# Moving the second MoE's weight conversion one half block later, and sixteen low-part subtractions from GpSimd to VectorE

## The chip, the core and the metric

The kernel runs on one core of a Trainium2 chip. The metric is device microseconds of one execution; lower is better.

## The reference

A linear attention feeds two MoE layers. There are 4 batches of 8 heads, 576 rows and 64 columns a head, which make 2304 tokens of 512 features; each MoE goes 512 to 2048 to 512.

```python
q_s = softmax(q, over the head's columns); k_s = softmax(k, over the rows)
x = q_s @ (k_s^T @ v)                          # per batch and head, then heads side by side
h = x @ moe_w_in;  g = where(h >= 1, h, where(h <= -1, 0, (h + 1)**2 / 4));  x = g @ moe_w_out
h = x @ moe2_w_in; g = h * tanh(log1p(exp(h)));                              out = g @ moe2_w_out
```

## The kernel before

The first MoE goes over the tokens in six blocks (0 to 5) of 384 columns. Each block has 16 slots, one for each 128 of the 2048 hidden features, so slots are counted from 0 to 95 through all blocks. In slot i TensorE makes gemm1 of feature group i (lines 496 to 498, 12 matmuls into a PSUM bank h) and gemm2 of group i - 3 (line 582, 12 matmuls into four banks acc). Block 0 multiplies in whole float32. From block 1 on each operand is split into a high part that is rounded and a low part that is the rest, and three products are summed. `act_scaled`, `act_squared` and `act_least` make g from h (ScalarE lines 539 and 543, VectorE line 548); `split_g` makes the high part of g on ScalarE (line 533) and the low part on the engine that `eltwise` names (line 534). There are two h banks, so gemm1 of group i waits until VectorE's line 548 has read group i - 2.

Beside this run four other streams. In block 1 `w_high` and `w_low` split the first MoE's weights (lines 237 and 242; the output weights' low part on GpSimd, the input weights' on VectorE). In blocks 1 to 4 a list of stages (`Fill`) makes the attention of the next block: transposes into qT, ScalarE's copy qt (line 460), and the product xps (line 467). The second MoE's weights are converted once, 32 items (2 matrices by 16 groups). An item is loaded (line 137 or 139), then goes through stages, one for each call of `w_tick`: `first` (two bit operations on VectorE, lines 151 and 155, two passes on ScalarE, 162 and 166), `second` (ScalarE line 170, and the product of line 183, on GpSimd for the input matrix and on VectorE for the output matrix); every second item goes on with `sums` (two additions on VectorE and one on GpSimd), `last_sum` (GpSimd) and `store` (four DMAs to DRAM, line 215, together 896 KB). `w_tick` takes a new item in two slots of three.

In block 5 (slots 80 to 95) the second MoE is made ready. The jobs of `ahead2` do, in this order of slots: 80 `x_load` of group 0 (four DMAs xq, line 665), 81 `x_sums` of group 0 (four additions of 128x768 on GpSimd), 82 `x_store` of group 0 (xk, line 676) and the fetch of converted weights of unit 0 (w, line 633), 83 `x_load` of group 1, 84 `x_sums` of group 1 and the next fetch of weights, 85 `x_store` of group 1 and the first operand (xf, line 685). Within a slot `w_tick` comes first, then gemm1, then these jobs, then `split_g` of the group before and the activations of this slot.

The order of instructions: SyncE, which issues the DMAs, and ScalarE keep the program's order everywhere. TensorE, VectorE and GpSimd are ordered by a planner in slots 16 to 79, and keep the program's order in slots 0 to 15 and from slot 80 on.

After block 5 the second MoE runs on the sums of a fast matrix scheme (lines 496 to 498 into m, then line 783 into o).

Of the kernel before, what the change touches and what calls it, by code (L numbers as in the profile page):

```python
# [63 lines left out]
def tile_attention_two_moes(  # L64
# [13 lines left out]
    nc = tc.nc  # L78
# [4 lines left out]
    NF = DFF // P  # L83
    NB = NT // TB
# [149 lines left out]
    def w_high(c, m):  # L234

        t = parts[c, m] = big([P, 2, DM], F32R, "parts")
        nc.scalar.activation(out=t[:, 0, :], in_=whole[m, c // 2][:, c % 2, :], func=AF.Copy)

    def w_low(c, m):
        t, w = parts[c, m], whole[m, c // 2][:, c % 2, :]  # L240
        eng = nc.gpsimd if m else nc.vector
        eng.tensor_tensor(out=t[:, 1, :], in0=w, in1=f(t[:, 0, :]), op=ALU.subtract)
# [260 lines left out]

    def eltwise(s):

        return nc.vector if s == slots[-1] else nc.gpsimd

    def gemm1(s):
        ph, n, c = s
        hs[s] = h_p.tile([P, 512], F32, tag="h", name="h")  # L510
        for kc in range(NP):
            ks = slice(kc * P, (kc + 1) * P)
            if n == 0:
                nc.tensor.matmul(
                    hs[s][:, :TB], whole[0, c // 2][:, c % 2, ks], xh[ph, n][kc // 2][:, kc % 2, :],
                    start=kc == 0, stop=kc == NP - 1,
                )
                continue
            three(
                hs[s][:, :TB], parts[c, 0][:, 0, ks], parts[c, 0][:, 1, ks],  # L520
                xh[ph, n][kc // 2][:, kc % 2, :], xl[ph, n][kc // 2][:, kc % 2, :], kc == 0, kc == NP - 1,
            )
# [4 lines left out]
    def split_g(s):  # L527
        if as_whole(s):
            return
        g = temps.pop(s)  # L530
        t = small([P, 2, TB], F32R, "ghl")
        gh[s], gl[s] = t[:, 0, :], t[:, 1, :]
        nc.scalar.activation(out=gh[s], in_=g, func=AF.Copy)  # L533
        eltwise(s).tensor_tensor(out=gl[s], in0=g, in1=f(gh[s]), op=ALU.subtract)  # L534
# [28 lines left out]
    def gemm2(s):  # L563
        ph, n, c = s
        first, last = c == 0, c == NF - 1
        key = s[:2]
        if first:
            acc[key] = [acc_p.tile([P, 512], F32, tag="acc", name="acc") for _ in range(NP)]
        if as_whole(s):
            for x, a in enumerate(acc[key]):  # L570
                nc.tensor.matmul(
                    a[:, :TB], whole[1, c // 2][:, c % 2, x * P:(x + 1) * P], gh[s], start=first, stop=last
                )
            del gh[s], hs[s]
            return
        woh, wol = parts[c, 1][:, 0, :], parts[c, 1][:, 1, :]

        order = [(x, at) for ats in ((0, 1), (2,)) for x in range(NP) for at in ats]
        for x, at in order:
            xs = slice(x * P, (x + 1) * P)  # L580
            pairs = [(woh[:, xs], gh[s]), (wol[:, xs], gh[s]), (woh[:, xs], gl[s])]
            nc.tensor.matmul(  # L582
                acc[key][x][:, :TB], *pairs[at], start=first and at == 0, stop=last and at == 2
            )
        del gh[s], gl[s], hs[s]
# [3 lines left out]
    def finish_block(ph, n):  # L589
        for e, a in enumerate(acc.pop((ph, n))):  # L590
            y = yp.tile([P, TB], F32, tag=f"y{e % 2}", name="y")
            if e % 2:
                nc.vector.tensor_copy(y, a[:, :TB])
            else:
                nc.scalar.activation(out=y, in_=a[:, :TB], func=AF.Copy)
            stores.append((yd[n][:, e, :], y))
# [301 lines left out]
    line = Line()  # L898
    fill = None

    def w_ahead():
        while ahead and len(raws) < 1:
            w_load(*ahead.pop(0))

    def w_tick(new):
        line.tick(w_stages(*todo.pop(0)) if todo and new else None)
# [46 lines left out]
    slots = [(1, n, c) for n in range(NB) for c in range(NF)]  # L953
# [7 lines left out]
    def slot(i):  # L961
        nonlocal fill
        s = slots[i] if i < len(slots) else None
        d = slots[i - LAG] if LAG <= i < len(slots) + LAG else None
        if s:
            ph, n, c = s
            if c == 0:
                fill = Fill(*plan.get((ph, n), ([], 1)))
            if (n > 1 or n == 1 and c >= NF // 2) and (n < NB - 1 or line.items):
                w_tick(i % 3)  # L970
                w_ahead()
            if n == 1:
                w = [(x, m) for x, m in ((c + AHEAD, 0), (c, 1)) if x < NF]
                for x, m in w:
                    w_high(x, m)
                for x, m in w:
                    w_low(x, m)
            gemm1(s)
        for job in ahead2.pop(i, []):
            job()  # L980
        while stores:
            nc.sync.dma_start(out=stores[0][0], in_=stores.pop(0)[1])
        for back in (1, 2, 0):
            if 0 <= i - back < len(slots):
                if back < len(acts) and i - back >= NF:
                    acts[back](slots[i - back])
        if fill:
            fill.step()
        if d:
            gemm2(d)  # L990
            if d[2] == NF - 1:
                finish_block(*d[:2])
        if fill:
            fill.step()
            if s and s[2] == NF - 1:
                fill.drain()
# [61 lines left out]
    for engines, upto in REGIONS:  # L1058
        with region(engines):
            for i in range(at, upto):  # L1060
                slot(i)
        at = upto
    with region(None):
        slot(len(slots) + LAG)
        for g in groups:
            for u in units:
                at = (g * len(units) + u) * per_unit
                for x, job in zip((2, 2, 5, 5), unit(g, u, places)):
                    if at + per_unit < end:
                        places.setdefault(at + per_unit + x, []).insert(0, job)  # L1070
                    else:
                        job()
        for at in range(len(products)):
            product(at, steps)
        assert not (todo or line.items or ahead2 or places or steps)
# [32 lines left out]
```

## Time and profile before

| | |
|---|---|
| median of 3 runs | 873.01 us (871.52 to 873.29) |
| the profiled execution | 872.6 us |
| its span, first to last instruction | 870.8 us |
| TensorE busy | 853.1 us (98% of the span) |
| VectorE, ScalarE, GpSimd busy | 563.0, 493.9, 400.5 us |

The profiled execution's own time is 1.8 us over its span and 0.4 us under the median. A matmul is counted as busy until its modelled end, and the next one starts before that, so the start times of matmuls tell more than the busy share.

### The profile page before, as it was taken

To read this page: it belongs to the slowest core of one execution; us is meant where nothing else is said; L and a number is where in the kernel's file an instruction comes from. 1 tells how busy PE (TensorE), PEld (TensorE's weight loads), DVE (VectorE), ACT (ScalarE), POOL (GpSimd) and SP (SyncE) were. 2 spreads that over 40 slices of the span, in tenths; PEclk is the share of its full clock that TensorE was granted. 3 is DMA by queue.
4 is the path that set the end of the run, shared out by engine and by line. 5 is a ranking of instruction groups with operands and counts; after the bars stand their busy time and mean duration, and the time that the engine had idled before them with its cause. 6 is when DMAs were issued, how large, how long until landed. Compare 5 with 4: busy or idle time off the path is not lost. (4 is left out here: it accounts for less than half of the span.)

```text
span 870.8 us, 14851 instructions
## 1 busy us (share of the span) xinstructions
PE 853.1 (98%) x5276; PEld 807.0 (93%) x5276; DVE 563.0 (65%) x907; ACT 493.9 (57%) x849; POOL 400.5 (46%) x373
## 2 busy tenths in 40 slices
PE   9999999989999999999999999999999999999998
PEld 9755769979999999999999999989999999999998
DVE  5899836686775775693147447755777679666453
ACT  2797986586676667784458434433433455553521
POOL 2454636496565355473374226558555467000000
PEclk9999999999999999999999999999999999999999
DMA  9999103225973755562187057687877897867833
GB/s 233 299 292 245 32 1 95 70 68 145 238 210 114 220 149 184 165 230 67 49 296 278 20 194 254 199 314 294 286 247 247 305 354 260 258 231 213 304 115 95
DMA packets 139995, 171.24 MB, mean 197 GB/s; under 512 B 57361, under 2 KB 109585, under 8 KB 139921
## 3 DMA queue, kind: packets, MB, share of 16 engines
q1 hardware_dynamic: 139680, 170.10, 61.6%
q8 instruction: 41, 0.67, 0.3%
q14 instruction: 34, 0.27, 0.1%
q10 hardware_dynamic: 240, 0.20, 0.1%
HBM read 108.40 MB, written 61.87 MB: 196 GB/s over the span
## 5 line engine op out<-in xcount | busy, mean ns | idle before, releaser
L582 PE MATMUL acc<-ghl,parts 128*128 128x384 f32 x960 | 183.0, 339 | 0.0
L582 PEld LDWEIGHTS acc<-ghl,parts 128*128 128x128 f32 x960 | 167.5, 188 | 1.1
L783 PE MATMUL o<-w2p,gc 128*128 128x256 f32 x1296 | 153.2, 280 | 1.7 <-ACT gc L624 1.7
L783 PEld LDWEIGHTS o<-w2p,gc 128*128 128x128 f32 x1296 | 152.5, 189 | 2.1 <-ACT gc L624 2.1
L534 POOL TENSOR_TENSOR ghl<-rg,ghl 128x384 fp32r<-128x384 f32 x79 | 87.9, 1114 | 99.8 <-ACT ghl L533 85.7
L548 DVE SCALAR_TENSOR_TENSOR rg<-h,rg 128x384 f32<-128x384 f32 x96 | 53.1, 553 | 105.2 <-ACT rg L543 92.2
L496 PE MATMUL h<-xh,parts 128*128 128x384 f32 x320 | 112.3, 351 | 0.5 <-DVE rg L548 0.5
L627 DVE TENSOR_TENSOR gc<-gq,gc 128x768 fp32r<-128x768 f32 x84 | 91.1, 1119 | 29.5 <-ACT gc L624 19.3
L497 PE MATMUL h<-xl,parts 128*128 128x384 f32 x320 | 108.0, 337 | 0.1
L498 PE MATMUL h<-xh,parts 128*128 128x384 f32 x320 | 107.9, 337 | 0.0
L624 ACT ACTIVATE gc<-gq 128x768 fp32r<-128x768 f32 x84 | 70.1, 843 | 63.6 <-DMA gq<-gd 43.1
L497 PE MATMUL m<-xc,w2p 128*128 128x384 f32 x288 | 97.7, 339 | 1.2 <-DVE xc L627 1.2
L496 PE MATMUL m<-xc,w2p 128*128 128x384 f32 x288 | 97.6, 339 | 1.0 <-ACT xc L624 1.0
L498 PE MATMUL m<-xc,w2p 128*128 128x384 f32 x288 | 97.5, 339 | 0.0
L539 ACT ACTIVATE rg<-h,half 128x384 f32<-128x384 f32 x96 | 55.5, 578 | 70.7 <-PE h L498 62.2
L720 ACT ACTIVATE high<-high 128x768 f32<-128x768 f32 x24 | 20.3, 847 | 95.7 <-DVE high L232 43.8
L155 DVE SCALAR_TENSOR_TENSOR wraw<-wraw 128x512 uint32<-128x512 uint32 x64 | 64.1, 1002 | 1.9
L232 POOL TENSOR_TENSOR s<-high 128x384 f32<-128x384 f32 x24 | 26.3, 1096 | 84.1 <-ACT high L720 84.1
L496 PEld LDWEIGHTS h<-xh,parts 128*128 128x128 f32 x320 | 60.5, 189 | 2.3 <-DVE rg L548 0.8
L497 PEld LDWEIGHTS h<-xl,parts 128*128 128x128 f32 x320 | 60.4, 189 | 1.9 <-DVE xl L479 0.4
L151 DVE TENSOR_SCALAR wraw<-wraw 128x512 uint32<-128x512 uint32 x64 | 40.7, 635 | 32.3 <-DMA wraw<-in_moe_w_out_dram 19.6
L498 PEld LDWEIGHTS h<-xh,parts 128*128 128x128 f32 x320 | 60.4, 189 | 0.0
(108 smaller groups left out, 1611.8 us busy)
## 6 DMA issues: line engine op xcount, KB each, us to landing
gq<-gd SPq DMA_DIRECT2D x84, 384.0 KB, 6.4
gd<-s SPq DMA_DIRECT2D x48, 384.0 KB, 3.3
wraw<-in_moe_w_in_dram SPq DMA_DIRECT2D x32, 512.0 KB, 5.9
wraw<-in_moe_w_out_dram SPq DMA_DIRECT2D x32, 512.0 KB, 5.5
gd<-low SPq DMA_DIRECT2D x24, 384.0 KB, 3.8
wk<-ws SPq DMA_DIRECT2D x32, 256.0 KB, 4.1
w<-wk SPq DMA_DIRECT2D x16, 384.0 KB, 4.2
v_t<-in_v_dram SPq DMA_DIRECT2D x32, 144.0 KB, 5.7
```

Source lines behind the costliest of these rows:

```text
L151: nc.vector.tensor_scalar(out=t[:, :, 0], in0=t[:, :, 0], scalar1=29, scalar2=0x40000000, op0=ALU.logical_shift_right, op1=ALU.bitwise_xor,)
L155: nc.vector.scalar_tensor_tensor(out=t[:, :, 0], in0=t[:, :, 1], scalar=3, in1=t[:, :, 0], op0=ALU.logical_shift_left, op1=ALU.bitwise_xor,)
L496: nc.tensor.matmul(ps, ah, bh, start=start, stop=False)
L497: nc.tensor.matmul(ps, ah, bl, start=False, stop=False)
L498: nc.tensor.matmul(ps, al, bh, start=False, stop=stop)
L534: eltwise(s).tensor_tensor(out=gl[s], in0=g, in1=f(gh[s]), op=ALU.subtract)
L539: nc.scalar.activation(out=t[:, 0, :], in_=hs[s][:, :TB], func=AF.Relu, scale=0.5, bias=half)
L548: nc.vector.scalar_tensor_tensor(out=g, in0=hs[s][:, :TB], scalar=1.0, in1=r, op0=ALU.max, op1=ALU.min)
L582: nc.tensor.matmul(acc[key][x][:, :TB], *pairs[at], start=first and at == 0, stop=last and at == 2)
L624: nc.scalar.activation(out=hi, in_=x, func=AF.Copy)
L627: eng.tensor_tensor(out=lo, in0=x, in1=f(hi), op=ALU.subtract)
L783: nc.tensor.matmul(ps[j][:, :QUARTER], a[:, c, js], b, start=i == c == which == 0 and b is wh, stop=i == pairs[-1] and c == which == 1,)
```

## The change

The low part of g in block 1 is made by VectorE (before: by GpSimd, as in all later blocks). The conversion of the second MoE's weights starts with slot 32, the first of block 2 (before: slot 24, the middle of block 1), and the slots that take no new item are those where i + 1 is a multiple of three (before: i). The 32 items so start in slots 33 to 79 (before: 25 to 71), and the stages of the last ones fall into slots 80 to 83 (before: up to slot 75).

```diff
     def eltwise(s):
-        return nc.vector if s == slots[-1] else nc.gpsimd
+        return nc.vector if s[1] == 1 or s == slots[-1] else nc.gpsimd
...
             if c == 0:
                 fill = Fill(*plan.get((ph, n), ([], 1)))
-            if (n > 1 or n == 1 and c >= NF // 2) and (n < NB - 1 or line.items):
-                w_tick(i % 3)
+            if n > 1 and (n < NB - 1 or line.items):
+                w_tick((i + 1) % 3)
                 w_ahead()
```

## Rows read from the trace of the kernel before

**Rows 1.** The page's first part: busy us, share of the span, instructions.
```profile
PE 853.1 (98%) x5276; PEld 807.0 (93%) x5276; DVE 563.0 (65%) x907; ACT 493.9 (57%) x849; POOL 400.5 (46%) x373
```

**Rows 2.** What TensorE waited for: us in total, times, longest.
```profile
PE xps L467 <- ACT qt L460: 4.3, 4, 3.1
```

**Rows 3.** TensorE's timeline, 189 to 210 us: start, us, operation, [idle before, releaser].
```profile
189.51 2.27 PE L582 MATMUL acc<-ghl,parts 128*128 128x384 f32 x12
194.93 1.65 PE L467 MATMUL xps<-qt,kvs 128*128 128x384 f32 x2 [3.14 <-ACT qt L460]
...
199.31 2.24 PE L582 MATMUL acc<-ghl,parts 128*128 128x384 f32 x12
201.40 0.33 PE L496 MATMUL h<-xh,parts 128*128 128x384 f32 x1
...
205.92 0.81 PE L467 MATMUL xps<-qt,kvs 128*128 128x384 f32 x2
...
208.66 1.56 PE L582 MATMUL acc<-ghl,parts 128*128 128x384 f32 x8
```

**Rows 4.** Windows: length, busy (instructions) by engine, granted clock, DMA share, GB/s.
```profile
196.00:198.00 2.00, 2.00 (x7) 1.70 (x7) 1.89 (x2) 0.89 (x2) 2.00 (x3) 0.50 0.60 219
```

**Rows 5.** Timelines of VectorE and ScalarE, 186 to 196 us.
```profile
186.69 3.37 DVE L155 SCALAR_TENSOR_TENSOR wraw<-wraw 128x512 uint32<-128x512 uint32 x1
...
190.09 0.68 ACT L162 ACTIVATE wraw<-wraw 128x512 f32<-128x512 f32 x1 [0.81 <-DVE wraw L155]
...
194.40 0.47 ACT L460 ACTIVATE qt<-qT 128x384 f32<-128x384 f32 x1
```

**Rows 6.** Groups of instructions by form, 125 to 207 us; last: the whole run's.
```profile
L155 DVE SCALAR_TENSOR_TENSOR wraw<-wraw 128x512 uint32<-128x512 uint32 x6 | 10.0, 1660 | 0.1
...
L534 POOL TENSOR_TENSOR ghl<-rg,ghl 128x384 fp32r<-128x384 f32 x15 | 17.1, 1139 | 0.0
...
L162 ACT ACTIVATE wraw<-wraw 128x512 f32<-128x512 f32 x5 | 3.3, 667 | 5.2 <-DVE wraw L155 5.2
...
L534 DVE TENSOR_TENSOR ghl<-rg,ghl 128x384 fp32r<-128x384 f32 x1 | 0.6, 557 | 0.7 <-ACT ghl L533 0.7
```

**Rows 7.** Windows of block 1 and block 2; columns as in rows 4.
```profile
125.00:207.00 82.00, 78.83 (x432) 73.13 (x431) 58.25 (x79) 55.49 (x106) 53.79 (x49) 0.98 0.25 74
207.00:282.00 75.00, 74.48 (x450) 73.14 (x449) 50.15 (x92) 52.58 (x95) 44.82 (x50) 1.00 0.69 187
```

**Rows 8.** SyncE's timeline, 376 to 470 us: when DMAs are issued.
```profile
398.28 1.10 SPq L215 DMA_DIRECT2D wk<-ws  x2
...
409.98 6.57 SPq L665 DMA_DIRECT2D xq<-yd  x4
...
440.79 0.99 SPq L633 DMA_DIRECT2D w<-wk  x2
441.88 2.16 SPq L665 DMA_DIRECT2D xq<-yd  x4
...
458.34 0.43 SPq L685 DMA_DIRECT2D xf<-yd  x1
```

**Rows 9.** GpSimd's timeline, 430 to 460 us.
```profile
432.76 7.63 POOL L232 TENSOR_TENSOR xq<-xq 128x768 f32<-128x768 f32 x4
...
449.29 8.65 POOL L232 TENSOR_TENSOR xq<-xq 128x768 f32<-128x768 f32 x4
...
457.90 2.19 POOL L534 TENSOR_TENSOR ghl<-rg,ghl 128x384 fp32r<-128x384 f32 x2
```

**Rows 10.** TensorE's timeline, 458 to 468 us.
```profile
458.45 2.25 PE L582 MATMUL acc<-ghl,parts 128*128 128x384 f32 x12
...
465.31 0.44 PE L496 MATMUL h<-xh,parts 128*128 128x384 f32 x1 [0.45 <-DVE rg L548]
```

**Rows 11.** Windows ahead of and in the burst of DMAs; columns as in rows 4.
```profile
418.00:432.00 14.00, 14.00 (x83) 14.00 (x82) 2.23 (x4) 5.45 (x11) 3.28 (x4) 1.00 0.06 24
440.00:454.00 14.00, 14.00 (x82) 14.00 (x81) 6.13 (x7) 7.38 (x16) 7.90 (x7) 1.00 1.03 366
```

## The prediction

> **What bounds the kernel now.** I read the page first: TensorE is busy for 853.1 of 870.8 us [rows 1], so what is to be won is TensorE's idle time and what follows from it. Next the list of what TensorE waited for: its largest entry is the attention's product xps waiting for ScalarE's copy qt, 4.3 us, of which one wait is 3.1 [rows 2]. Next the timeline there. Twelve matmuls of gemm2 take 201.40 - 199.31 = 2.09 us [rows 3], so one takes 0.174 and a slot of 24 takes 4.18. The twelve that start at 189.51 could be followed at 191.60; xps started at 194.93, which is 3.33 us lost. From xps to the next gemm2 it then took 199.31 - 194.93 = 4.38 us, where the next slot needs 208.66 - 205.92 = 2.74 for the same work [rows 3]: another 1.64, and in this stretch the granted clock is 0.50, the lower of TensorE's two levels, 1.2 GHz [rows 4]. The place has cost 3.33 + 1.64 = 4.97 us. It lies in slot 30, in the half block that converts weights before the change.
>
> Why qt was late is in the other engines' timelines. One bit operation of a conversion (line 155) took 3.37 us on VectorE [rows 5], against 1.66 in the mean of block 1 [rows 6]. ScalarE, which keeps the program's order, waited 0.81 for it and reached qt only at 194.40 [rows 5]. In block 1 ScalarE waits 5.2 us in all for line 155 [rows 6]. So this wait comes from conversions, which stand ahead of qt in ScalarE's order. Block 2 converts too and has no such hole: TensorE is busy for 74.48 of 75 us [rows 7]; block 1 differs in that the first MoE's weights are split at the same time.
>
> **The change, part by part.** *Out of block 1.* Slots 25, 26, 28, 29 and 31 no longer take an item. That removes five `first` stages and four `second`, and two `sums`, among them line 155's 10.0 us and ScalarE's 5.2 us of waiting for it [rows 6]. With nothing of this in front of it, qt follows its transpose as in slot 31, whose xps shows no wait [rows 3]. I take all 4.97 us as won. The bounds are nothing, if ScalarE is late for another reason, and 4.97.
>
> *The subtraction on VectorE.* One of this form on VectorE takes 0.557 us, those of block 1 on GpSimd 1.139 [rows 6]. Sixteen add 8.9 us to VectorE, whose 58.25 us in block 1 [rows 7] lose at least line 155's 10.0. So VectorE stays at 57.2 us of a block that takes 82.0 - 5.0 = 77: cost 0, hidden by TensorE's matmuls. The upper bound is that each also waits for one whole GpSimd subtraction: 16 x (0.557 + 1.139) = 27.1 and 75.4 of 77, which is still less, though with little left. In order on VectorE, what would wait behind a late subtraction is line 548, and gemm1 for it by way of the h bank. GpSimd loses 17.1 us and gains nothing.
>
> GpSimd is busy for 53.79 of block 1's 82 us [rows 7], so line 155 mostly had GpSimd work beside it, and its 3.37 against 1.66 fits two engines in each other's way. The Trainium skill (SBUF — State Buffer, "SBUF: two separate sides") says that a VectorE operation with two inputs in SBUF and a GpSimd operation lock each other out of a shared pair of ports for a whole instruction. By that rule the moved subtractions are not at 0.557 but near the upper bound above, and the time would come out as in the fifth case below; by the row of 0.557, a single one, it would not.
>
> *Into blocks 2 to 4.* The same conversions run there as before, in other slots. Blocks 2 to 4 keep their density; only slots 72 to 79 get work that they did not have, with an attention that is nearly done. Cost 0, hidden as in block 2 [rows 7]; the nearest row for a small new wait is 0.45 us [rows 10], so I keep 1.5 us either way for three blocks.
>
> *Into block 5.* The last item now starts in slot 79. Its product falls into slot 80, its `sums` into 81, `last_sum` into 82 and its four stores into 83, where no engine can run them early, since from slot 80 on all keep the program's order. There the trace has no slack. DMA goes from a share of 0.06 ahead to 1.03 at 366 GB/s from 440 to 454 us [rows 11]. The order on SyncE is: fetch of weights at 440.79, `x_load` of group 1 at 441.88 [rows 8]; GpSimd's `x_sums` of group 1 from 449.29 to 457.9, and behind it two subtractions [rows 9]; the operand xf at 458.34, behind the stores of these sums [rows 8]; and gemm1 of slot 88 at 465.31, already 0.45 late for line 548, which follows in ScalarE's order on the conversion of xf [rows 10]. So what the end of `x_sums` of group 1 loses, TensorE loses in full. The first subtraction behind it ends near 459.0 (half of 2.19 after 457.90 [rows 9]) and is needed after eight matmuls of the gemm2 at 458.45, at 459.84 [rows 10]: there 0.85 is spare.
>
> How late does it get? The item's addition on GpSimd stands ahead of `x_sums` of group 0, which starts at 432.76 [rows 9]. It is 128x256; an addition of 128x768 takes 7.63 / 4 = 1.9 us [rows 9], so it costs between a third of that, 0.6, and 1.9. I take 1.0, nearer to its size than to the larger one's. By it the stores and the fetch behind shift. Then the four stores of the item go ahead of `x_load` of group 1 on SyncE: 128 x 7 x 256 x 4 bytes = 0.917 MB, by 366 GB/s 2.5 us in a stretch that is full [rows 11]. `x_sums` can begin when the first two of four loads have landed, so between 0 and 2.5 of this shows; I take half, 1.2. `last_sum` stands behind `x_sums` of group 0, but the stores' turn on SyncE comes after that anyway. In sum 2.2 us come back, bounds 0.6 and 4.4.
>
> *The first load.* `x_load` of group 0 is issued at 409.98 before [rows 8]. It now stands behind the loads and stores of the last items. The last store before is issued at 398.28 [rows 8]; in the code it is in slot 75, whose gemm2 lies 11 slots before the one at 458.45 (slot 86), at 458.45 - 11 x 4.18 = 412.5. So such steps run some 14 us ahead of TensorE. The store in front of this load is in slot 80, whose gemm2 lies at 433.4; it would go at some 420 to 424, and 1.57 MB take 4.3 us at 366 GB/s: landed by 430, before `x_sums` at 432.76. Cost 0; that it comes late is the fourth case.
>
> **Sum.** -4.97 + 0 + 0 + 2.2 = -2.8 us. From the profiled execution's 872.6 that is 869.8; it lies 0.4 below the median of 873.0, so for the median I forecast 870.2. Faster and slower mean by over 0.2%, 1.75 us, about what a measurement of this kernel can tell from no change.
>
> **The cases.**
> 1. The forecast: the hole in slot 30 is gone, and block 5 takes 2.2 back; 870.2, with its own range 868.9 to 871.5. Chance 0.43.
> 2. The burst swallows the stores, because DMA catches up later: only 0 to 1 us comes back, 868.0 to 869.0. For it: `x_sums` starts right behind GpSimd's earlier work, so the loads may have landed earlier than needed. Against it: the share of 1.03 [rows 11]. Chance 0.20.
> 3. The change does only half of what it says: ScalarE reaches qt late in block 1 for the weights' split, and half of the hole stays: 873.0 - 2.5 + 2.2 = 872.7. For it: ScalarE's own 55.49 us there are mostly the split and the activations [rows 7]. Against it: the first half of block 1 has the split without a hole in the list of waits [rows 2]. Chance 0.14.
> 4. Slower: `x_load` of group 0 is issued only at its own place, at the start of slot 80, 433.4 - 2.1 = 431.3. It lands at 435.6, `x_sums` starts 2.8 later than now, and with the stores' 2.5 behind it block 5 gives back 5.3; a wait of over 3 us was followed by the lower clock, 1.64 more [rows 3, 4]: 873.0 - 5.0 + 5.3 + 1.6 = 874.9. It decides from a landing after 435.3 on. Against it: the stores run ahead as shown above. Chance 0.13.
> 5. Slower by another road: VectorE is the bound of block 1. Each subtraction is held up by a GpSimd operation as in the upper bound, line 548 gets late again and again, and as much is lost as is won: 873.0 + 2.2 = 875.2. It decides once VectorE has more than 77 us to do there. Against it: 75.4 at worst. Chance 0.10. (This is what the Trainium skill's rule on the shared ports would bring.)
>
> Faster by over 0.2%: nearly all of the first two, 0.62. Within: most of the third and some of the first and fourth, 0.20. Slower: 0.18. The range that leaves out no more than 2 in 10 goes from 867.5, a little under the second case for the small waits of blocks 2 to 4, to 873.8, past the third.
>
> **What would show it.** In block 1: no wait of xps for qt of more than 0.5 us, no stretch at 0.50, line 155 absent, line 534 on VectorE with a mean that says by how far it is held up (0.56 or near 1.7), and some 77 us in place of 82. In blocks 2 to 4: busy TensorE as now. In block 5: stores wk between the fetch of weights and `x_load` of group 1, `x_sums` of group 1 some 2 us later against gemm2, waits in slots 86 and 88 that together are some 2.2 us longer than the 0.45 there now. What would make it wrong: a wait of qt or of an h bank in another block, put there by the conversions' new slots, or a lower clock after the waits of block 5.

## The result, and the profile after

The changed kernel takes 877.3 us (876.25 to 877.95, 5 runs) where the kernel before takes 873.01 (870.4 to 874.14, 5 runs): a ratio of 1.0056, interval [1.0043, 1.007]. It is slower by 4.3 us; the forecast was 870.2, range 867.5 to 873.8. The profiled execution took 877.04 us, with a span of 875.3.

The page's first part answers to [rows 1]:

```profile
PE 855.0 (98%) x5276; PEld 808.3 (92%) x5276; DVE 567.3 (65%) x923; ACT 492.6 (56%) x849; POOL 384.4 (44%) x357
```

VectorE gained sixteen instructions and 4.3 us, GpSimd lost sixteen and 16.1 us. Nothing here says why the time is longer. The list of what TensorE waited for (us in total, times, longest) says more, beside [rows 2]:

```profile
PE xps L467 <- ACT qt L460: 4.1, 4, 1.7
...
PE acc L582 <- POOL ghl L534: 1.9, 1, 1.9
...
PE h L497 <- DVE xl L479: 1.0, 1, 1.0
```

The wait for qt has the same sum as before, but its longest part is 1.7 in place of 3.1: these are other waits. First the old place, slot 30, in TensorE's timeline (start, us, operation, idle before and releaser), the answer to [rows 3]:

```profile
189.22 2.28 PE L582 MATMUL acc<-ghl,parts 128*128 128x384 f32 x12
191.34 0.81 PE L467 MATMUL xps<-qt,kvs 128*128 128x384 f32 x2
...
194.09 2.24 PE L582 MATMUL acc<-ghl,parts 128*128 128x384 f32 x12
```

Here xps starts 2.12 us after gemm2, with no wait, and the next gemm2 starts at 194.09 against 199.31 [rows 3]: 5.22 us earlier. So I took the start of each slot's gemm2 in both traces and followed the difference, after minus before, through the kernel:

| start of gemm2 in slot | 32 | 47 | 48 | 64 | 80 | 88 | 95 |
|---|---|---|---|---|---|---|---|
| after minus before, us | -5.22 | -1.97 | -1.06 | +0.39 | +1.52 | +5.41 | +5.46 |

Blocks 2 to 4 lose 1.52 + 5.22 = 6.74 us, block 5 another 5.46 - 1.52 = 3.94. (Behind slot 95 about 1 us is regained; in that part, whose instructions are the same, the runs below differ from the kernel before by -3.5 to +2.5 us, worked out as the difference of the spans less that at slot 95, so the stages are compared up to slot 95 and the kernels by their medians.) Within blocks 2 to 4 the loss comes in steps: 3.25 at slot 45, 0.91 at 48, 2.0 at 54 to 56, 1.0 at 71.

The windows of after (length, busy by engine in the order PE, PEld, DVE, ACT, POOL, then granted clock, DMA share, GB/s) answer to [rows 7] and show what a busy share can't:

```profile
125.00:207.00 82.00, 82.00 (x461) 77.29 (x461) 57.10 (x86) 49.87 (x98) 30.13 (x27) 1.00 0.20 53
...
207.00:282.00 75.00, 73.13 (x433) 71.15 (x432) 46.50 (x87) 48.06 (x89) 41.24 (x46) 0.98 0.57 155
```

In the window of block 2 (which begins about one slot later in the block than before) VectorE, ScalarE and GpSimd are all less busy than before (50.15, 52.58 and 44.82 [rows 7]), and TensorE is nevertheless idle for 75 - 73.13 = 1.87 us (0.52 before). That does not look like a lack of room. What it is stands in the timelines of slots 44 and 45. VectorE, with two rows of GpSimd (POOL) at its end, then ScalarE, then TensorE (the later rows are slots 56 and 71):

```profile
257.38 0.16 DVE L363 TENSOR_SCALAR den<-kv 128x2 f32<-128x2 f32 x1 [0.80 <-PE kv L351]
257.45 0.53 DVE L151 TENSOR_SCALAR wraw<-wraw 128x512 uint32<-128x512 uint32 x1
...
258.01 0.69 DVE L155 SCALAR_TENSOR_TENSOR wraw<-wraw 128x512 uint32<-128x512 uint32 x1
...
260.85 1.51 DVE L151 TENSOR_SCALAR wraw<-wraw 128x512 uint32<-128x512 uint32 x1 [0.93 <-DMA wraw<-in_moe_w_in_dram]
262.40 1.48 DVE L155 SCALAR_TENSOR_TENSOR wraw<-wraw 128x512 uint32<-128x512 uint32 x1
263.91 0.56 DVE L548 SCALAR_TENSOR_TENSOR rg<-h,rg 128x384 f32<-128x384 f32 x1
...
261.06 1.02 POOL L534 TENSOR_TENSOR ghl<-rg,ghl 128x384 fp32r<-128x384 f32 x1
262.29 1.04 POOL L183 TENSOR_TENSOR wq<-wraw 128x512 f32<-128x512 f32 x1 [0.21 <-ACT wraw L170]
```

```profile
258.74 0.69 ACT L162 ACTIVATE wraw<-wraw 128x512 f32<-128x512 f32 x1 [3.54 <-DVE wraw L155]
...
261.12 0.53 ACT L543 ACTIVATE rg<-rg 128x384 f32<-128x384 f32 x1
...
264.50 0.53 ACT L533 ACTIVATE ghl<-rg 128x384 fp32r<-128x384 f32 x1 [2.29 <-DVE rg L548]
...
265.96 0.47 ACT L460 ACTIVATE qt<-qT 128x384 f32<-128x384 f32 x1
...
322.25 0.67 ACT L162 ACTIVATE wraw<-wraw 128x512 f32<-128x512 f32 x1 [3.55 <-DVE wraw L155]
...
391.11 0.68 ACT L162 ACTIVATE wraw<-wraw 128x512 f32<-128x512 f32 x1 [4.28 <-DVE wraw L155]
```

```profile
264.52 0.44 PE L496 MATMUL h<-xh,parts 128*128 128x384 f32 x1 [0.53 <-DVE rg L548]
...
266.48 1.48 PE L467 MATMUL xps<-qt,kvs 128*128 128x384 f32 x2 [1.34 <-ACT qt L460]
...
268.08 0.52 PE L496 MATMUL h<-xh,parts 128*128 128x384 f32 x1
...
325.58 0.92 PE L467 MATMUL xps<-qt,kvs 128*128 128x192 f32 x4 [1.71 <-ACT qt L460]
...
394.43 0.91 PE L467 MATMUL xps<-qt,kvs 128*128 128x384 f32 x2 [0.79 <-ACT qt L460]
```

Read it from the bottom up. xps waits for qt, which ScalarE makes at 265.96, behind line 533, which waited 2.29 us for VectorE's line 548. Line 548's input was there at 261.12 + 0.53 = 261.65, but it ran at 263.91: in VectorE's order the two bit operations of the next conversion (lines 151 and 155) stand ahead of it, and the first of them sat still for 0.93 us until its weights had landed. Then the two took 1.51 and 1.48 us, where those of the item before took 0.53 and 0.69: GpSimd was at work beside them, and each ended 0.28 and 0.55 us behind an operation of GpSimd (262.08 and 263.33). In e2 and e11, which have the same order here, line 151 waited 0.75 and 0.52 us for its load, took 1.70 and 1.92, and again ended 0.29 us behind GpSimd's line 534; so within these executions GpSimd, and not the landing, set when it ended. One item earlier line 548 was not concerned, but ScalarE was: line 155 at 258.01 stands behind the attention's den, which waits for the product kv, and ScalarE, in the program's order, waits 3.54 us for it in line 162. Slots 56 and 71 also show 3.55 and 4.28 us of ScalarE behind line 155, then a late qt. TensorE's waits in slot 45 sum to 0.53 + 1.34 = 1.87; most of the rest of its 3.25 is the clock: matmuls that take 0.52 us, as in the row at 268.08, in place of 0.33 [rows 3].

Block 5: SyncE's issues, GpSimd, ScalarE, TensorE, in place of [rows 8 to 10]:

```profile
443.85 0.99 SPq L633 DMA_DIRECT2D w<-wk  x2
444.89 0.48 SPq L215 DMA_DIRECT2D wk<-wq  x1
445.46 0.90 SPq L215 DMA_DIRECT2D wk<-ws  x2
446.42 0.46 SPq L215 DMA_DIRECT2D wk<-wq  x1
446.97 3.26 SPq L665 DMA_DIRECT2D xq<-yd  x4
```

```profile
434.97 0.75 POOL L232 TENSOR_TENSOR ws<-wq 128x256 f32<-128x256 f32 x1
435.68 7.77 POOL L232 TENSOR_TENSOR xq<-xq 128x768 f32<-128x768 f32 x4
...
454.12 8.29 POOL L232 TENSOR_TENSOR xq<-xq 128x768 f32<-128x768 f32 x4 [1.38 <-DMA xq<-yd]
462.36 1.97 POOL L534 TENSOR_TENSOR ghl<-rg,ghl 128x384 fp32r<-128x384 f32 x2
```

```profile
460.06 0.63 ACT L624 ACTIVATE w2p<-w 128x512 fp32r<-128x512 f32 x1 [5.15 <-DMA w<-wk]
```

```profile
459.94 1.57 PE L582 MATMUL acc<-ghl,parts 128*128 128x384 f32 x8
463.41 0.97 PE L582 MATMUL acc<-ghl,parts 128*128 128x384 f32 x4 [1.91 <-POOL ghl L534]
464.77 0.69 PE L496 MATMUL h<-xh,parts 128*128 128x384 f32 x1 [0.39 <-DVE rg L548]
...
468.46 2.27 PE L582 MATMUL acc<-ghl,parts 128*128 128x384 f32 x12
```

For the wait of 1.91 us the road is the forecast one: the four stores wk go ahead of `x_load` of group 1, `x_sums` of group 1 waits 1.38 us for its loads, the subtraction behind it is late, and gemm2 of slot 86 waits for it. The wait of 0.39 is not that of slot 88 in [rows 10], which is gone, but gemm1's of slot 87, and it has a road of its own: the next fetch of weights is issued at 453.07 (before: 447.37, so 4.18 later against slot 80), ScalarE waits 5.15 us for these weights (line 624), and behind that in its order stand the activations that line 548 needs. What the forecast did not price is what follows: that gemm1 lasts 468.46 - 464.77 = 3.69 us, where twelve matmuls take 2.09 [rows 3], at a granted clock of 0.67 and 0.50, the latter the lower level (1.2 GHz). These are windows of after there; before, both showed 1.00:

```profile
464.00:466.00 2.00, 1.61 (x7) 1.29 (x6) 1.76 (x3) 0.12 (x1) 0.33 (x1) 0.67 0.99 281
466.00:468.00 2.00, 2.00 (x8) 2.00 (x7) 0.00 (x0) 0.21 (x1) 0.00 (x0) 0.50 0.93 266
```

### The profile page after: what moved, and what is told of

Same layout as the page of the kernel before. It is cut to its first block, busy times and chain, and to the rows that moved or that the text cites. A ratio compares the mean times of both kernels' runs of the same rounds, so it can differ in the third digit from the quotient of the medians.

```text
span 875.3 us, 14832 instructions
## 1 busy us (share of the span) xinstructions
PE 855.0 (98%) x5276; PEld 808.3 (92%) x5276; DVE 567.3 (65%) x923; ACT 492.6 (56%) x849; POOL 384.4 (44%) x357
## 4 chain that ended last, share of the span: by engine, by line
PE 66%; DMA 8%; DVE 8%; issue 6%; ACT 6%; POOL 5%; SPq 1%; POOLq 0%; DVEq 0%; ACTq 0%
PE o L783 18%; PE acc L582 12%; PE h L496 4%; PE h L498 4%; PE h L497 4%; POOL s L232 4%; PE m L497 3%; PE m L498 3%; PE acc L571 3%; PE m L496 3%; PE h L514 3%; PE warm L944 2%; DMA wraw<-in_moe_w_in_dram 2%; PE kv L351 2%; DMA q_t<-in_q_dram 2%
## 5 line engine op out<-in xcount | busy, mean ns | idle before, releaser
L534 POOL TENSOR_TENSOR ghl<-rg,ghl 128x384 fp32r<-128x384 f32 x63 | 68.6, 1090 | 93.1 <-ACT ghl L533 92.8
L162 ACT ACTIVATE wraw<-wraw 128x512 f32<-128x512 f32 x64 | 41.7, 681 | 31.9 <-DVE wraw L155 24.0
```

The source lines that it names most:

```text
L162: nc.scalar.activation(out=sg, in_=sg, func=AF.Copy, bias=ROUND)
```

## The experiments

Fourteen kernels were run. "Blocks 2 to 4" is the change of the difference to before from slot 32's gemm2 to slot 80's, "block 5" that from slot 80's to slot 95's, as worked out above; a plus is a loss. Each ratio is to runs of the kernel before that were taken together with that kernel (their medians go from 871.84 to 873.01). The last two columns come from the one profiled execution, which is not the median one: it lies over the median by 5.3 us in e7, 2.8 in e2 and 1.9 in e8, and under it by 1.3 in e13 and e14.

| kernel | median us | ratio to before, interval | blocks 2 to 4 | block 5 |
|---|---|---|---|---|
| the change | 877.3 | 1.0056 [1.0043, 1.007] | +6.7 | +3.9 |
| e1_lows_only | 869.88 | 0.997 [0.996, 0.9981] | +0.8 | -0.5 |
| e2_slots_only | 879.53 | 1.0085 [1.0052, 1.0117] | +9.4 | +3.9 |
| e3_phase0 | 874.83 | 1.003 [1.0012, 1.0049] | +2.5 | +2.4 |
| e4_phase2 | 869.05 | 0.9969 [0.9956, 0.9982] | +1.8 | -0.1 |
| e12_phase2_gpsimd | 869.45 | 0.9971 [0.9957, 0.9985] | +2.2 | +0.1 |
| e5_hold_store | 875.42 | 1.0046 [1.0031, 1.0061] | +5.9 | +1.5 |
| e6_hold_all | 876.42 | 1.0056 [1.0041, 1.0071] | +6.0 | +1.7 |
| e7_early_phase1 | 880.15 | 1.01 [1.0083, 1.0117] | +10.1 | -0.2 |
| e8_one_item | 876.23 | 1.0046 [1.0024, 1.0068] | +5.6 | +3.5 |
| e9_two_items | 871.36 | 0.9983 [0.9966, 1.0] | +3.8 | +3.6 |
| e10_tick_last | 870.88 | 0.9976 [0.9959, 0.9992] | -0.5 | +3.9 |
| e11_phase2_tick_last | 878.6 | 1.0072 [1.0047, 1.0098] | +5.0 | +3.4 |
| e13_four_items | 868.23 | 0.9948 [0.9929, 0.9967] | -1.0 | +2.9 |
| e14_four_items_hold | 867.38 | 0.9939 [0.9923, 0.9956] | -1.0 | +1.9 |

The changed kernel, e2, e5, e6 and e11 run the same instructions in blocks 2 to 4, and in the same order on VectorE and TensorE. They lose 6.7, 9.4, 5.9, 6.0 and 5.0 us there. So much comes from one execution to the next, mostly from falls of TensorE's clock, of about 1.6 us each (last section): two in e2, one in the changed kernel, none in the other three.

**The two halves of the change alone.** e1 is the kernel before with VectorE's subtractions, e2 the changed kernel without them.

```diff
     def eltwise(s):
-        return nc.vector if s == slots[-1] else nc.gpsimd          # e1: before
+        return nc.vector if s[1] == 1 or s == slots[-1] else nc.gpsimd
...
-        return nc.vector if s[1] == 1 or s == slots[-1] else nc.gpsimd   # e2: after
+        return nc.vector if s == slots[-1] else nc.gpsimd
```

> The kernel before with one part of the change: VectorE makes the low parts of g in block 1, the conversions stay in slots 25 to 71. If the waits of the changed kernel in blocks 2 to 4 (some 6.5 us) come from the moved conversions, this stays within 1.5 us of the kernel before, 871.5 to 874.5, with the hole of slot 30 there in some size. If they come from the subtractions on VectorE, which change the planned order, waits show up in blocks 2 to 4 and the time is 876 or more.

> The changed kernel without its first part: GpSimd makes all low parts, the conversions run in slots 33 to 79. If slots alone matter: the hole of slot 30 is gone, blocks 2 to 5 lose what they lose in the changed kernel, 876 to 879. If the subtractions on VectorE cause the waits in blocks 2 to 4: these are gone, and 870 to 872 remains, with block 5's 3.9 us alone.

e1 wins 0.3% (it lies under its expected 871.5 to 874.5), e2 loses 0.85%: the loss belongs to the slots. VectorE's line 155 of e1 in 125 to 207 us answers to [rows 6], xps in slot 30 to [rows 3]:

```profile
L155 DVE SCALAR_TENSOR_TENSOR wraw<-wraw 128x512 uint32<-128x512 uint32 x6 | 6.6, 1107 | 0.1
```

```profile
194.57 0.91 PE L467 MATMUL xps<-qt,kvs 128*128 128x384 f32 x2 [2.30 <-ACT qt L460]
```

Taking GpSimd's subtractions away, with the conversions still in block 1, brings line 155 from a mean of 1.66 [rows 6] to 1.11 us, and slot 30 gives back 2.39 of its 4.93: xps waits 2.30 us in place of 3.14, and the clock stays at 1.00 there. So both parts of the change work on the same hole, but only the 0.84 us of shorter waiting can be put down to the subtractions; the rest is the fall of the clock that e1 does not have, and such a fall comes in one execution and not in another.

**Other slots for the same items.** e3 and e4 take the items in other slots of three (the first load is put ahead of block 2); e12 is e4 with the subtractions on GpSimd.

```diff
-                w_tick((i + 1) % 3)
+                w_tick(i % 3)              # e3
+                w_tick((i + 2) % 3)        # e4, e12
                 w_ahead()
+            if i == 31:
+                w_ahead()
```

> The changed kernel with the free slots at i a multiple of three (the first load is issued in slot 31). If the waits of blocks 2 to 4 come from which conversion meets which stage of the attention, they move: no hole of 3.3 us in slot 45, sum of blocks 2 to 4 between 0 and 6 and other than 6.5 by over 1, time 871 to 876; block 5 loses 3 to 4 as in the changed kernel. If the denser work of blocks 2 to 4 itself is the cause, the sum stays 5.5 to 7.5 and the time 876 to 879.

> The changed kernel with the free slots at i + 2 a multiple of three, so that the last item starts in slot 78 and its store falls into slot 82. If meeting stages is the cause: another sum for blocks 2 to 4 than 6.5 and than with the other pattern, by over 1 us. If density is the cause: 5.5 to 7.5 again. In block 5 the stores then stand ahead of the stores and loads of slot 82, so a loss of 1 to 4 us there.

> The run with free slots where i + 2 is a multiple of three, without the subtractions on VectorE. If these cost or gain little by themselves, 868 to 870.5. If they help by taking work from GpSimd in block 1, where slot 30's hole has gone in either case, a loss of 1 us or more shows in block 1 or early in block 2, 870.5 to 872. If VectorE's order is what they change, blocks 2 to 4 lose another sum than 1.75, by over 1 us either way.

Shifted by one slot or two, the same 32 items lose 2.5 or 1.8 us in blocks 2 to 4 in place of 6.7, and e4 beats both kernels. In e4 the last stores are issued by 431.8 us, ahead of the stores of group 0 and of the fetch of weights (from 432.78), and block 5 loses nothing, where 1 to 4 us were expected. e4 and e12 are equal, so the subtractions on VectorE cost nothing once the conversions are out of block 1.

**Block 5: the stores, then the additions too.** e5 holds the last item's stores to slot 91; e6 also its additions.

```diff
-            if n > 1 and (n < NB - 1 or line.items):
+            if n > 1 and (n < NB - 1 or line.items and (i < 83 or i > 90)):   # e5
+            if n > 1 and (n < NB - 1 or line.items and (i < 81 or i > 90)):   # e6
```

> The changed kernel, with the last item's four stores held from slot 83 to slot 91; its additions stay where they are. If the stores' 0.9 MB ahead of the load of group 1 cause block 5's loss of 3.9 us, that falls to 1.4 or less (what the additions on GpSimd leave), and the time is 873 to 875. If the additions on GpSimd cause it, it stays at 3 or more and the time at 876 to 878.

> The changed kernel, with the last item's additions and stores both held to slots 91 to 93. Block 5's loss is 0.5 us or less by either reading, and the time 872.5 to 874.5; the difference to the run that holds the stores alone is what the additions cost, up to 1.4 us. If it stays at 3 or more, the loss came in with the last stores and the product in slot 80, or with the time at which block 5 begins.

GpSimd's timeline of e5 has `x_sums` of group 1 here:

```profile
451.94 8.65 POOL L232 TENSOR_TENSOR xq<-xq 128x768 f32<-128x768 f32 x4
```

and ScalarE's of e6 has the conversion of xf that gemm1 of slot 88 hangs on:

```profile
465.93 0.84 ACT L624 ACTIVATE xc<-xf 128x768 fp32r<-128x768 f32 x1 [4.50 <-DMA xf<-yd]
```

With slot 80 at +1.52 in both, `x_sums` of group 1 is late by 454.12 - 449.29 - 1.52 = 3.31 us in the changed kernel and by 451.94 - 449.29 - 1.52 = 1.13 in e5; the stores are worth 2.2. In e6 it starts at 451.53 with slot 80 at +1.87, so 0.37 late: the additions are worth about 0.8. Block 5 falls from 3.9 to 1.5 in e5, and of these 2.4 us 1.6 are the fall of the clock, which e5 does not have there. e6 brings nothing more: at most 0.5 was expected to be left, and 1.7 is. Its gemm1 of slot 88 waits 2.1 us for line 548, which stands behind ScalarE's conversion of xf: from the issue at 460.60 to ScalarE's use it takes 5.33 us, before 462.38 - 458.34 = 4.04. Why xf lands later stays open. Neither run touches the 6 us of blocks 2 to 4.

**Does a slot make its hole?** e7 is e1 with the changed kernel's slots of three, but from block 1 on.

```diff
             if (n > 1 or n == 1 and c >= NF // 2) and (n < NB - 1 or line.items):
-                w_tick(i % 3)
+                w_tick((i + 1) % 3)
                 w_ahead()
+            if i == 23:
+                w_ahead()
```

> The kernel before with VectorE's subtractions and with the changed kernel's free slots, i + 1 a multiple of three, from slot 24 on (first load in slot 23). Its items end in slot 71, so block 5 loses nothing. If meeting stages sets the waits of blocks 2 to 4, items in the same slots as the changed kernel's meet the same stages, and the holes of slots 45 and 56 come back in part (2 us or more together); time 870 to 874. If the shift by a half block itself made them, blocks 2 to 4 lose under 1 us and the time is that of the run with the subtractions alone, 869 to 871.

Neither of its expectations came true. The holes did not stay where the slots stayed: slots 44 to 46 lost 0.4 in place of 3.2, slots 48 and 49 5.5 in place of 0.9, and slots 33 to 41 some 3.4 that the changed kernel does not lose there; block 1, with the conversions in it, lost another 2. The profiled execution took 885.4 us, the other four 879.8 to 880.9, and its mean granted clock is 0.57 both from 196 to 204 and from 295 to 303 us, so these sizes are not typical: some 3.4 us of the 5.5 are the clock. Which item meets which part of the attention counts too, not the slot alone.

**One item out of the way, then two.** In e8 the item of slot 43 is taken in slot 44, the free one; in e9 also that of 48 in 50.

```diff
-                w_tick((i + 1) % 3)
+                w_tick((i + 1) % 3 if i not in (43, 44) else i == 44)                    # e8
+                w_tick((i + 1) % 3 if i not in (43, 44, 48, 50) else i in (44, 50))      # e9
```

> The changed kernel with one item of the 32 taken in slot 44 in place of slot 43. VectorE's planned order changes in some 15 instructions there: line 548 of two slots comes ahead of the bit operations (lines 151 and 155) that stood in front of it. If that order makes the hole of slot 45, its 3.25 us go to 1 or less, the other holes (slots 48, 56, 71, 87) stay within 0.5 us, and the time is 873.5 to 875. If ScalarE is late there for the amount of work, the hole stays above 2.

> The run with one moved item, with a second one moved: the item of slot 48 is taken in slot 50, so that VectorE's order has the low part of x that gemm1 of slot 48 needs ahead of the bit operations, which waited 2.6 us there for their load. If that order holds up TensorE, the hole of slots 48 and 49 (3.8 us in the run with one moved item) goes to 1 or less, and the time is 871.5 to 874. If the late xps or the amount of work on VectorE and ScalarE makes it, it stays above 2.5, or as much comes up within the next six slots.

In e8 slot 45's hole is gone (a step of -0.76), but slots 48 and 49 lose 3.8. VectorE and TensorE of e8:

```profile
282.52 0.43 DVE L151 TENSOR_SCALAR wraw<-wraw 128x512 uint32<-128x512 uint32 x1 [2.60 <-DMA wraw<-in_moe_w_in_dram]
...
283.80 0.55 DVE L479 TENSOR_TENSOR xl<-xps,xh 128x384 fp32r<-128x384 f32 x1
```

```profile
284.40 0.44 PE L497 MATMUL h<-xl,parts 128*128 128x384 f32 x1 [2.32 <-DVE xl L479]
```

VectorE waits 2.60 us for one item's weights, with the activations' low part xl behind them in its order, TensorE waits 2.32 for xl, and the clock falls. This hole need not come from the item that was moved: with the changed kernel's own order TensorE waits for xl there 0.99, 2.08 (e2), 1.68 (e5), 1.76 (e6) and 0.75 us (e11), and e2 loses 3.5 in slots 48 and 49. e8's 876.23 lies above the expected 873.5 to 875. e9 moves that item, and this hole is gone as well: 6 us less in the median than the changed kernel's, with two of 32 items moved. Slots 54 to 57 lose 3.8 there (2.0 in the changed kernel): xps waits 1.94 in place of 1.71, and the clock falls.

**Order within a slot.** e10 and e11 call the tick at the end of a slot, on the changed kernel and on e4.

```diff
-            if n > 1 and (n < NB - 1 or line.items):
-                w_tick((i + 1) % 3)
-                w_ahead()
...
             fill.step()
             if s and s[2] == NF - 1:
                 fill.drain()
+        if s and n > 1 and (n < NB - 1 or line.items):
+            w_tick((i + 1) % 3)          # e10; e11: (i + 2) % 3
+            w_ahead()
```

> The changed kernel with w_tick and w_ahead called at the end of a slot, behind the activations and the stages of the attention, in place of ahead of them. The same work, in the same slots. If the holes of blocks 2 to 4 come from conversions standing ahead of line 548, qt and the low parts of x in the order of ScalarE and VectorE, their sum falls from 6.5 us to 2.5 or less; block 5's stores then go behind the load of group 1 and its loss falls to 2 or less; time 866 to 872. If it is the amount of work, the sum stays above 5 and the time above 874.

> The same edit on the run whose free slots are those with i + 2 a multiple of three, which lost 1.75 us in blocks 2 to 4. By the order's reading 866 to 869, no slower than that run's 869.05; and if order is what matters, the two patterns now differ by under 3 us in blocks 2 to 4, where they differed by 5. By the reading of work, 868 to 872 and no change.

This pair does not test what it was made for. The end of a slot is the start of the next one, so e11 has the changed kernel's slots again, and its holes (1.67 at slot 45, 0.66 at 48, 2.0 at 54 to 56, 1.1 at 71); e10 has e3's slots, one item later. As such they are two more patterns: e3 loses 2.5 us in blocks 2 to 4, e10 nothing. For block 5 e10 does tell something. Its last stores go behind `x_load` of group 1, so `x_sums` of group 1 does not wait for its loads, and yet the block loses 3.9, where at most 2 was expected:

```profile
457.84 0.45 PE L496 MATMUL h<-xh,parts 128*128 128x384 f32 x1 [1.96 <-DVE rg L548]
```

The stores (443.22 to 447.01) are now ahead of the next fetch of weights, issued at 447.29; ScalarE waits 5.67 us for it, line 548 is late, gemm1 of slot 87 waits, and the clock falls behind it. So behind `x_load` they hold up another urgent transfer.

**Four items, and the stores.** e13 moves two more items, from slot 55 to 56 and from 70 to 71. e14 is e13 with e5's held stores.

```diff
-                w_tick((i + 1) % 3)
+                w_tick((i + 1) % 3 if i not in (43, 44, 48, 50, 55, 56, 70, 71) else i in (44, 50, 56, 71))
```

> The kernel with items moved from slots 43 to 44 and 48 to 50, and two more: from 55 to 56 and from 70 to 71, each into the next slot that takes none. Theory (a hole belongs to the bit operations of one item that stand ahead of a copy, a low part or line 548 in the order of VectorE and ScalarE, and goes with that item): the step of slots 56 and 57, 3.8 us with two items moved, falls to at most 1, that of slot 71 from 1.1 to at most 0.3, block 5 keeps its 3.5 to 3.9; the time is some 867 to 869 us. Rival (work that the slots lack room for: a hole only moves on): slots 50 to 80 lose as much in other slots, and the time stays at 871 or above.

> The four items moved and, as in the run that held the last item's stores until slot 91, these stores out of block 5's way. Theory: blocks 2 to 4 as with four items moved, block 5 loses at most 1.7 in place of 3.5 to 3.9: 865 to 867.5 us, which is the hole of slot 30 won (5) and little given back. Rival: the moved items open holes elsewhere, 869 or above.

The list of e13's waits has this left of qt, and TensorE's timeline this in place of the 1.34 us:

```profile
PE xps L467 <- ACT qt L460: 0.2, 1, 0.2
```

```profile
264.37 0.81 PE L467 MATMUL xps<-qt,kvs 128*128 128x384 f32 x2
```

VectorE's order at slots 44 and 45, the changed kernel's (-) against e13's (+):

```
 L367 TENSOR_TENSOR kvs_87<-kv,den 64x2x64 x2
 L412 TENSOR_REDUCE qm<-q_t 96x8
-L151 TENSOR_SCALAR wraw<-wraw 128x512
-L155 SCALAR_TENSOR_TENSOR wraw<-wraw 128x512
-L548 SCALAR_TENSOR_TENSOR rg<-h,rg 128x384
+L548 SCALAR_TENSOR_TENSOR rg<-h,rg 128x384
+L151 TENSOR_SCALAR wraw<-wraw 128x512
```

Line 548 now stands ahead of the bit operations. The same work, with four items in another slot, loses nothing in blocks 2 to 4 (a change of -1.0), no hole moved on, and e13 is 0.52% under the kernel before. In e14 block 5 gives back 1.9, a little over the 1.7 expected and 1.0 less than in e13 (the clock falls in neither), and the kernel takes 867.38 us, 0.61% under the kernel before: the lowest median of all, though its interval overlaps e13's. Room was not what blocks 2 to 4 lacked.

## Why the prediction was wrong, point by point

- **The hole in slot 30: right.** Forecast -4.97; the steps at slots 27 and 30 sum to -5.2, and twelve of the fourteen runs, those that have the conversions out of block 1, show the same -4.93 at slot 30. The two that keep them there (e1, e7) don't.
- **The subtraction on VectorE at no cost: right, though not at 0.557 us.** The sixteen take 16.3 us, a mean of 1.022, between the two bounds. Nine began while GpSimd was at work on line 242 and took 1.35 to 1.46 us, seven did not (or in its last 0.06 us) and took 0.50 to 0.55 (one of the nine stands in the last section). The Trainium skill (SBUF — State Buffer, "SBUF: two separate sides") has a VectorE operation with two inputs in SBUF and a GpSimd operation that reads SBUF lock each other out for a whole instruction. These sixteen agree: GpSimd held VectorE up. The time does not follow in block 1: VectorE is busy 57.10 of 82 us in the window, and e4 and e12 are equal. The fifth case did not come. (The 10.0 us of line 155 that the forecast took off VectorE are six operations, and the sixth, 1.50 us, is slot 32's and stays; it changes no term.)
- **"Into blocks 2 to 4": this step failed.** "Blocks 2 to 4 keep their density … Cost 0, hidden as in block 2", with 1.5 us either way. It cost 6.7, and 5.0 to 9.4 in the five executions with this order. Density was indeed kept; the error is that a busy share was taken for a cover. By the timelines, what decides is what stands ahead of line 548, qt and xl in the orders of VectorE and ScalarE, and what these wait for: a bit operation behind kv, behind its own load, or held up by GpSimd. Line 162 waited 24.0 us for line 155 from 207 to 430 us, and 23.2 in the kernel before, so ScalarE waits hardly more than it did, 8 times in place of 11. Nor does the length of a wait decide by itself: e4 has two of over 5 us in this line, and loses 1.8 in these blocks. The bound of 1.5 came from the nearest small wait (0.45 [rows 10]), though the trace held a better row for this very thing: the 3.33 us of slot 30, a conversion ahead of qt [rows 3, 5]. That it could happen in another block stood among the things that would make the prediction wrong, with no price.
- **Block 5: the right place, half the size.** Forecast 2.2 (bounds 0.6 to 4.4), measured 3.9. The waits are 1.91 + 0.39 against 0.45, 1.85 more. The rest is mostly the clock: gemm1 of slot 87 took 3.69 in place of 2.09, 1.60 more. That the waits come near 2.2 is in part luck, for the split of the 2.2 was off: counted by how late `x_sums` of group 1 starts, the additions are worth 0.8 (taken as 1.0), the stores 2.2 (taken as 1.2, half of a transfer time). And TensorE does not lose "in full" what the end of `x_sums` loses: that end is 462.41 - 457.94 - 1.52 = 2.95 late, the waits grew by 1.85. The late fetch of weights, a second road into the same place, was not in the forecast. The stores' price was in [rows 8]: two of them take SyncE 1.10 us to issue, so four take 2.2, and the next load is issued that much later; in the changed kernel the next load follows the first store by 446.97 - 444.89 = 2.08 us.
- **The first load: right.** `x_load` of group 0 was issued at 426.17; `x_sums` of group 0 started right behind the addition, without a wait. The fourth case did not come.

So -5.2 + 6.7 + 3.9 = +5.4 up to slot 95, against -5.0 + 0 + 2.2; the spans differ by 875.3 - 870.8 = 4.5. None of the five cases had it.

Shown by the runs is that the slots of four items out of 32 make the 6.7 us (e13), and the timelines show the order through which they do. No run changed the order alone: a moved item has its load and its passes on ScalarE at another time as well. In block 5 the stores are shown to take part, but not to be most of the loss: holding them gives back 2.4 in e5, of which 1.6 is the clock, and 1.0 in e14 against e13; 1.5 to 1.9 are left, and in e6 these come mostly from a late xf. What stays open is why the planner orders line 548 behind the bit operations in one pattern and ahead of them in another; its own due times were not varied. Nor is it shown that each of the four holes needs just the item that was moved for it.

## What to carry to other kernels

A queue that keeps an order hides work only if nothing urgent stands behind it: when work is moved under a busy engine, look at what stands next in each engine's order behind every operation that may wait (for a load, for a product, for GpSimd), and price it with the worst wait of this kind that the trace already has, not with the mean load of the block. When moved background work can start in several patterns of slots, run them all: here the same items went from -1.0 to +6.7 us in three blocks, and over that in single executions. And a DMA issued ahead of an urgent one cost that one, here, the time that its queue took to issue it: 2.08 us for four.

## What the runs showed that was not expected

TensorE's clock falls after short waits, and not always. In slot 45 the changed kernel waited 0.53 and 1.34 us with two matmuls between, and the clock fell; e5, whose instructions differ only in block 5, waited 0.55 and 1.34 in the same place and its clock stayed. The windows 268 to 270 us of the changed kernel, and then of e5:

```profile
268.00:270.00 2.00, 2.00 (x7) 2.00 (x7) 0.84 (x3) 0.73 (x2) 1.19 (x2) 0.50 0.00 0
```

```profile
268.00:270.00 2.00, 2.00 (x13) 1.86 (x12) 1.70 (x5) 1.57 (x3) 0.32 (x1) 1.00 0.00 0
```

Seven matmuls against thirteen in 2 us: the step at slot 45 was 3.25 in the one and 1.67 in the other, so one such fall cost 1.6 us, and the same waits brought it in one execution and not in the other. In block 5 the clock fell after 1.91 and 0.39 us in the changed kernel, and stayed at 1.00 in e13 after a wait of 2.04 and in the gemm1 behind it. Elsewhere it fell after single waits of 1.94 (e9, slot 56), 2.08 (e2, slot 48) and 2.32 us (e8, slot 48), and stayed after 2.10 (e6, slot 88) and 2.30 (e1, slot 30). The windows of e13:

```profile
456.00:458.00 2.00, 1.54 (x7) 1.22 (x8) 1.17 (x3) 0.77 (x2) 1.36 (x2) 1.00 1.05 309
458.00:460.00 2.00, 2.00 (x13) 2.00 (x12) 0.59 (x1) 0.30 (x1) 0.00 (x0) 1.00 0.96 347
```

The forecast had met the lower clock only behind a wait of over 3 us [rows 3, 4].

GpSimd's hold on VectorE also came out more sharply than a mean shows. In the traces of all sixteen kernels from 125 to 430 us, line 155 took 0.68 to 0.70 us each of the 336 times that no operation of GpSimd was under way when it began (or one in its last 0.1 us), and 1.39 in the median, 3.37 at most, the 176 times that one was. One of the nine subtractions of block 1 in the changed kernel that met one, behind the GpSimd operation beside it:

```profile
130.09 1.28 POOL L242 TENSOR_TENSOR parts<-whole,parts 128x512 fp32r<-128x512 f32 x1 [4.85 <-ACT parts L237]
130.39 1.40 DVE L534 TENSOR_TENSOR ghl<-rg,ghl 128x384 fp32r<-128x384 f32 x1 [0.24 <-ACT ghl L533]
```

There it cost TensorE nothing that shows. In slot 45 it is 1.77 us in the two bit operations ahead of line 548, against those of the item before; and in slot 30 of the kernel before, the line 155 of 3.37 us [rows 5] had GpSimd operations beside it all the time.
